# One list of single operations through QKV and W1, tails read by one DMA, and 15 more warm-up transposes

## The chip, the cores and the metric

The kernel runs on one core of one Trainium2 chip. The metric is device time in microseconds (us), the median of several executions. A profiled execution has a span (first to last instruction) and its own time, which is a little longer than the span.

## The reference

S = 2048 tokens, D = 576, F = 4608, all in float32. Two branches read one normalized input and are summed:

```python
xn = _layernorm(x)
return x + _A_ref(xn, A_wqkv, A_wo) + _B_ref(xn, B_w1, B_w2, B_w3, B_w4)
# _A_ref: 32 heads of 18, each token attends to itself and 7 earlier ones, 2 apart
qkv = x @ wqkv                    # 576 -> 1728
o = softmax(q . k * scale) . v    # window of 8, dilation 2
return o @ wo
# _B_ref: spatial shift, then an MLP
h = gelu(layernorm(x) @ w1)       # 576 -> 576, four groups of 144 columns
hs = concat(h[:, g0] shifted +1, g1 shifted -1, g2 shifted +2, g3 shifted -2) @ w2
x1 = x + hs
return x1 + gelu(layernorm(x1) @ w3) @ w4
```

## The kernel before

The stages follow one another on TensorE: QKV, W1 with its GELU, W2, then the MLP (W3 and W4 in turns, with the attention in the background on VectorE), and Wo. A float32 product is made of rounded parts: each operand is split into a high part (ScalarE, a cast) and a remainder (VectorE, a subtraction), and high x high, high x low and low x high are accumulated. D = 576 is four blocks of 128 rows and a tail of 64, or two halves of 288 with tails of 32; the high and low of a tail share one block, so a tail is wanted several times over, at several partitions.

*QKV.* Token tiles 0 to 5 (128 tokens each) go by `unit`, plain products of one tile with 432 columns of `wqkv`: 24 units of 14 matmuls. Each tile is loaded (`x`), its statistics are taken (`st`), it is normalized (`no`, L168), its tails are copied (`ta`, L342), it is turned by TensorE (`tm`, `tt`; L350, L354) and split out of PSUM (`ch`, `cl`, `ct`, `cu`; L553 to L559). The weights come by `load_cg` (`c0.0` to `c3.2`; L304 the halves, L308 the tails), and are split (`wh`, `wl`, `wL`, `wt`, `wu`, `wU`; L323, L326, L524, L528; a capital means GpSimd makes the remainder). Tiles 6 to 15 go in pairs, by 7 products in place of 8 on a 2 x 2 split (`g`, L701); their sums of weight blocks are `sb` (L333), and each pair is turned by VectorE (`zt`), put to memory (`zp`), read back by `get_pair` (`gp`) and split (`sx`, `ph`, `pl`, `pt`, `pu`).

All of this is one string of tokens, `ORDER_Q`. Each token issues the few instructions of one operation, and the loop over it sets each engine's program order. An engine runs its own queue in order, so a token's place matters against the others of its engine. SyncE issues the loads and stores here. Its eight DMA semaphores go round: a DMA waits until the one issued eight before it has landed.

*W1.* After the list stands a loop written by hand: for each of four blocks of 512 tokens, `mix_tile` for each of four column groups (14 matmuls, L785; two GELUs, L790 and L791; the remainder, L792), and `mix_rem`, 9 matmuls for the 64 columns left over (L800), which are copied out (L803), swapped between partitions by eight small DMAs (L805, L806), and placed with their shifts. The normalized blocks lie in memory as `zt`. A ring of two buffers holds them in SBUF; `get_z` loads a block's main rows (L187) and its tail rows (L190), and `split_x` splits it (L218 to L225). Blocks 0 and 1 are loaded from the list. Blocks 2 and 3 are loaded by

```python
            if b + 2 < NB and i == 4:
                get_z(b + 2, ring_block(("z", b + 2)))
```

as the last thing of block b, once its buffer is free. The loop also loads and splits `w2` (L765, L769, L237, L238) and, by `back`, returns five token tiles to SBUF (L656).

*Warm-up.* At the start TensorE turns the identity 24 times (L456), while the first loads are under way.

Of the kernel before, what the change touches and what calls it, by code (L numbers as in the profile page):

```python
# [53 lines left out]
x0 st0 x1 st1 x2 c0.1 st2 no0 ta0 tm0 c0.0 c0.2 x3 c2.0 no1 tm1 no2 c2.1 c2.2 wh0B11.1 wL0B11.1  # L54
wh0B11.0 wl0B11.0 ch0 tt0 ct0 tm2 x4 x5 ch1 st3 u0.0 u1.0 u1.1 cl1 u1.2 zpad cu0 cl0 no3 ta2
wt0B11 wU0B11 ta1a ch2 cl2 tt1 ta3 wh0B12.0 tt2 ct2 ct1 cu1 u0.2 u0.1 u0.3 st4 u0o u0s u1.3 tm3
ch3 cu2 aw3 no4 st5 c1.0 c1.2 c1.1 tt3 ct3 cu3 u2.0 u2.1 x9 tm4 ta4 u1o u1s cl3 wl0B12.0 wt0B12
u2.2 u2.3 u2o ch4 no5 u3.0 u3.1 u2s wh0B12.1 wl0B12.1 x6 u3.2 u3.3 u4.0 u3o u5.0 aw2 tt4 ct4 u3s
u4.1 u4.2 wu0B12 aw1 sb0.0 sb0.1 wh1B11.0 wh1B11.1 tm5 ch5 sc0 u4.3 u4o x7 ta5 wt1B11 u5.1 u5.2 x8
u5.3 u4s u5o u5s sb0.2 wt0T3 sb0.3 st6 no6 u6.0 u6.1 u6.2 u6.3 u6o u6s u7.0 u8.0 u8.1 tt5 u7.1  # L60
u7.2 u7.3 cl4 u8.2 cu4 cl5 u8.3 wh0T3.1 st7 st9 u7o u9.0 st8 wh0T3.0 u9.1 u7s ct5 cu5 u9.2 u9.3
wh0T1.0 u8o u10.0 u9o wl1B11.0 u8s u9s u10.1 u10.2 u10.3 u10o wu0T3 u11.0 u11.1 u11.2 wh0T1.1
u11.3 wl0T3.0 u11o wl1B11.1 u11s u12.0 u12.1 wt0T1 wu1B11 u12.2 u12.3 u12o u13.0 u13.1 u13.2 u10s
no7 wl0T3.1 sc2 wl0T1.1 c3.0 c3.1 wl0T1.0 wu0T1 u14.0 u14.1 u13.3 sc6 u14.2 c3.2 u14.3 u12s early
zg6 zt6 zg7 u13o u15.0 u15.1 u15.2 u15.3 sc8 u13s zt7 zp3.2 wh1B12.0 wh1B12.1 zp3.1 wl1B12.0
wl1B12.1 u14o u16.0 u16.1 u14s wt1B12 zp3.0 zp3.3 sb1.0 wu1B12 sb1.1 sb1.2 sb1.3 u15o u16.2 u15s
wh1T1.0 u17.0 u16.3 u16o wl1T1.0 wh1T3.0 no8 u16s u17.1 u17.2 u18.0 u18.1 u17.3 u17o u18.2 u17s
u18.3 u18o u18s u19.0 u19.1 zg8 zt8 no9 zg9 zt9 u19.2 u19.3 u20.0 u20.1 u20.2 gp3.0 gp3.1 gp3.2
u19o wt1T3 gp3.3 gp3.4 wu1T3 gp3.5 sx3.0 u20.3 u21.0 u21.1 u20o u22.0 wh1T3.1 zp4.0 u21.2 zp4.3
zp4.1 zp4.2 u19s u21.3 pt3A12 pu3A12 u21o ph3A11 pt3A22 pt3A11 sx3.1 sx3.3 ph3S4 pu3A11 pu3A22  # L70
u22.1 u20s u22.2 u22.3 ph3S1 pl3A11 sx3.2 pt3S4 pu3S4 u23.0 u23.1 ph3A22 pl3A22 u23.2 ph3A12 u21s
ph3S3 pl3A12 pl3S4 x10 u23.3 gp4.0 gp4.1 pt3S3 pu3S3 pl3S3 wt1T1 wu1T1 pl3S1 pt3S1 pu3S1 wl1T3.0
wl1T3.1 wh1T1.1 wl1T1.1 st10 x11 st11 no10 gp4.2 gp4.3 gp4.4 u22o u22s gp4.5 sx4.0 u23o u23s mid
g6.1 g6c g7.1 g7c g6.5 g7.5 g6.2 ph4A11 pl4A11 g6o2 g6s2 sx4.2 ph4A12 aw0 g6.6 g6k5 g6k6 g7k5 g7.6
g7k6 g6.7 g6o7 sc10 g6s7 zg10 g6.3 x12 sx4.1 ph4S1 no11 zt10 zg11 g6o3 zt11 zg0 zp5.1 zp5.0 zp5.2
g6.4 g6o4 pt4A11 sc4 g7.7 g6s4 pl4S1 g7o7 zt0 pu4A11 pt4S1 zg1 zt1 pt4A12 pu4A12 sx4.3 g7.3 g7.2
g7o2 g7.4 g7o4 g8.1 g9.1 pu4S1 g8c g8.5 g7o3 g9.5 pt4A22 ph4A22 pu4A22 pt4S3 pl4A22 pl4A12 zg2
zp5.3 zt2 x13 st13 g8.2 st12 sc12 zp0.0 g9c g6s3 g8.6 ph4S3 pl4S3 g8o2 g8k5 g8k6 zp0.1 g7s7 g9k5
g9.6 g9k6 zp0.2 pu4S3 zp0.3 g8s2 no12 no13 g9.3 g9o3 zg12 zt12 zg13 zt13 gp5.0 g8.3 gp5.1 ph5A11
pl5A11 ph5A22 gp5.2 gp5.3 gp5.4 pt5A11 gp5.5 g9.7 pt5A12 g8.7 g9o7 g8o7 g7s4 g7s2 ph5A12 sx5.0 x14  # L80
sx5.1 ph5S1 pu5A12 g9.2 g8.4 x15 g8o4 aw4 g9.4 zp6.1 zg3 pu5A11 g9o2 g9o4 g7s3 pl5A12 zp6.0 g10.1
g11.1 sx5.2 pl5S1 pt5S1 zp6.3 zp6.2 g8s4 g8s7 zt3 zp1.3 g9s7 g8o3 pu5S1 g10c g10.6 st15 g11c g11.6
g8s3 sx5.3 ph5S3 g10.5 st14 sc14 gp6.0 gp6.1 no15 gp6.2 gp6.3 pt5A22 gp6.4 gp6.5 pl5A22 g9s2 no14
# [12 lines left out]
gz1.4 w1l1 g14s4 gz1.5 g15s4 gz1.0 w1h2 gz1.1 gz1.2 gz1.3 g15o3 z0u g15s3 w1h3 w1l3 g14s7 w1l2
# [8 lines left out]
def fused_block(ctx, tc, x, wqkv, wo, w1, w2, w3, w4, out):  # L105
# [75 lines left out]
    def get_z(b, xt, part=None):  # L181
        raw = xt.bitcast(F32)
        for i in range(6):
            if part in (None, i):
                src, c = zt[2 * b + i % 2], slice(256 * (i % 2), 256 * (i % 2) + 256)
                if i > 3:
                    sp.dma_start(raw[:, 5:9, c], src[0:512].rearrange("(k p) c -> p k c", p=128))  # L187
                else:
                    a = 64 * (i // 2)
                    sp.dma_start(raw[a:a + 64, 4, c], src[512:576])  # L190
# [108 lines left out]
    def load_cg(cg, raw, parts=(0, 1, 2)):  # L299
        r = qraw[cg] = raw() if qraw.get(cg) is None else qraw[cg]  # L300
        c = cg * QB
        for k in range(2):
            if k in parts:
                sp.dma_start(r[:, k, 1:3, :], wqkv[HF * k:HF * k + 256, c:c + QB]  # L304
                             .rearrange("(s p) c -> p s c", p=128))
        if 2 in parts:
            for a in range(0, 128, 32):
                sp.dma_start(r[a:a + 32, :, 0, :],  # L308
                             dram_ap(wqkv, 256 * 3 * D + c,
                                     [[3 * D, 32], [HF * 3 * D, 2], [1, QB]]))  # L310
# [62 lines left out]
    def get_pair(p, part):  # L373
        if part < 2:
            k = part
            sp.dma_start(raw_x(p, k)[:, 1:3],
                         dram_ap(zt[p], HF * k * 256, [[256, 128], [128 * 256, 2], [1, 256]]))
        else:
            a = 32 * part - 64
            raw = pair_x(p).bitcast(F32)[:, 0, 512:1024].rearrange("p (k c) -> p k c", k=2)  # L380
            sp.dma_start(raw[a:a + 32],
                         dram_ap(zt[p], 256 * 256, [[256, 32], [HF * 256, 2], [1, 256]]))
# [71 lines left out]
    warm = psa.tile([128, 512], F32, name="p1", tag="a")  # L454
    for i in range(24):
        pe.transpose(warm[:, :128], ident, ident)  # L456
# [38 lines left out]

    for u in range(24):
# [157 lines left out]
    def back():  # L654
        for t in range(5):
            sp.dma_start(Y[:, t, :], ysp[t])  # L656

    for i in range(6):
        add(f"gz0.{i}", lambda i=i: get_z(0, ring_block(("z", 0)), i))
        add(f"gz1.{i}", lambda i=i: get_z(1, ring_block(("z", 1)), i))  # L660

    def split_z(what):
        xt = xring["z", 0]
# [15 lines left out]
    for w in ("t", "u", "h0", "l0", "h1", "l1"):  # L679
        add(f"z0{w}", split_z, w)  # L680
# [59 lines left out]
    for name in ORDER_Q.split():  # L740
        T[name]()
    psq.__exit__(None, None, None)
    open_ab()
    q2p.__exit__(None, None, None)
    qp.__exit__(None, None, None)


    mp = tc.tile_pool(name="mp", bufs=1, reuse_waits="tile")
    mpool = mp.__enter__()
    W2 = mpool.tile([128, 10, D], F32R, name="W2")  # L750
    H = [[mpool.tile([128, S + 4], F32R, name=f"h{p}{g}") for g in range(4)] for p in range(2)]
# [1046 lines left out]
```

## Time and profile before

| | us |
|---|---|
| median of three runs | 1264.47 (1262.1 to 1265.52) |
| profiled execution, its own time | 1261.03 |
| its span | 1259.3 |
| TensorE busy in the span | 1241.0 |
| QKV on TensorE, from the first product matmul | 12.8 to 181.2 |
| W1 | 181.2 to 247.0 |
| W2 and all that follows | 247.0 to the end |
| mean granted TensorE clock | 0.997 |

In a timeline a row is a start, a duration, the engine, the line, the instruction, and in brackets how long the engine stood idle before it and what ended that. SPq is SyncE's queue of DMA issues. Overlapping matmuls are merged, so a group's duration over its count is the step from one to the next. In the table of windows each row is a stretch, its length, and then the busy us and instruction counts of TensorE's matmuls, its weight loads, VectorE, ScalarE and GpSimd, the granted clock, the DMA engines' share and GB/s.

### The profile page before, as it was taken

Reading aid. Unit: us, or ns where it says so; the run is one execution under the profiler, and the core shown is the slowest. Engines: PE = TensorE matmul, PEld = TensorE weight load, DVE = VectorE, ACT = ScalarE, POOL = GpSimd, SP = SyncE. Lnnn points to the kernel's source line nnn. Section 1 sums busy time; section 2 is a strip of 40 time slices with the busy share of each in tenths; the row PEclk is TensorE's granted clock in tenths of the full one; section 3 lists DMA queues with packets and bytes.
Section 4 is the critical chain, followed back from the end, with each engine's and each line's share of the span. In section 5 each row is a group of like instructions: output and inputs, shape, how many; then the busy total and the mean of one; then the engine's idle time right before and its main releaser. Section 6 shows DMA issues by size and latency. Waiting matters only on the chain.

```text
span 1259.3 us, 19957 instructions
## 1 busy us (share of the span) xinstructions
PE 1241.0 (99%) x7346; PEld 1141.6 (91%) x7346; DVE 932.4 (74%) x1182; ACT 759.8 (60%) x1234; POOL 278.7 (22%) x415
## 2 busy tenths in 40 slices
PE   8999999999999999999999999999999999999998
PEld 7999997799898999999899998999989999999898
DVE  6877645678458999997759998989989893554441
ACT  4556565526545545455867777776676776676620
POOL 5503100021222211212223232222122232222200
PEclk8999999999999999999999999999999999999999
DMA  8778993356888986769678898888968769899972
GB/s 221 178 181 200 196 236 111 116 155 177 207 226 183 222 159 145 158 137 246 124 174 188 196 186 210 180 167 212 258 114 186 141 128 199 182 210 232 261 241 78
DMA packets 221130, 230.50 MB, mean 183 GB/s; under 512 B 99544, under 2 KB 158136, under 8 KB 220904
## 3 DMA queue, kind: packets, MB, share of 16 engines
q1 hardware_dynamic: 188280, 162.43, 45.7%
q0 software_dynamic: 32752, 66.80, 32.8%
q8 instruction: 58, 0.95, 0.3%
q14 instruction: 40, 0.33, 0.1%
HBM read 130.76 MB, written 108.82 MB: 190 GB/s over the span
## 4 chain that ended last, share of the span: by engine, by line
PE 65%; DMA 3%; ACT 1%; DVE 1%; issue 1%; SPq 0%; POOL 0%; ACTq 0%; DVEq 0%; POOLq 0%
PE ps L1192 31%; PE cc L1456 19%; PE p L1156 10%; PE ps L252 4%; DMA w3st<-in_B_w_dram 1%; DMA yd<-ev 1%; DMA x1n<-xd 1%; DMA yd<-Y 1%; DVE xt L917 0%; SPq L1492 0%; PE p L1765 0%; DVE Y L1203 0%; ACT Y L1197 0%; ACT Y L1136 0%; DVE w3st L1289 0%
## 5 line engine op out<-in xcount | busy, mean ns | idle before, releaser
L1192 PEld LDWEIGHTS ps<-w,c 128*128 128x128 f32 x3456 | 477.8, 189 | 18.4 <-ACT Y L1197 2.9
L1192 PE MATMUL ps<-w,c 128*128 128x288 f32 x3456 | 487.8, 296 | 3.0 <-ACT Y L1197 1.6
L1198 POOL DMA_DIRECT2D yd<-Y x154 | 138.9, 905 | 369.8 <-ACT Y L1197 315.7
L1147 DVE TENSOR_TENSOR c<-Y,c 128x512 fp32r<-128x512 f32 x144 | 98.9, 687 | 89.2 <-ACT Y L1136 84.4
L1197 ACT COPY Y<-ps 128x576 f32<-128x576 f32 x154 | 97.9, 636 | 74.3 <-PE ps L1192 63.9
L1456 PE MATMUL cc<-xt,w3s 128*128 128x512 f32 (+1 forms) x504 | 127.2, 392 | 0.0
L1456 PEld LDWEIGHTS cc<-xt,w3s 128*128 128x128 f32 (+1 forms) x504 | 92.3, 188 | 17.3
L1200 ACT COPY Y<-ps 128x576 f32<-128x576 f32 x89 | 57.0, 640 | 59.4 <-PE ps L1192 58.0
L1067 DVE TENSOR_TENSOR po<-q,k 128x1152 f32<-128x1152 f32 (+1 forms) x48 | 84.2, 1755 | 0.8
L1070 DVE TENSOR_REDUCE L<-po 128x64 f32<-128x1152 f32 (+1 forms) x48 | 84.0, 1751 | 0.8
L1456 PE MATMUL cc<-x1n,w3a 128*128 128x512 f32 (+1 forms) x336 | 84.6, 392 | 0.0
L1135 ACT ACTIVATE c<-p 128x512 fp32r<-128x512 f32 x48 | 28.7, 598 | 86.3 <-PE p L1156 86.3
L1043 DVE TENSOR_TENSOR po<-v,L 128x1152 f32<-128x1152 f32 x56 | 75.4, 1354 | 0.9
L1466 DVE TENSOR_TENSOR Y<-cc,Y 128x512 f32<-128x512 f32 x49 | 33.7, 688 | 55.4 <-ACT Y L1462 49.7
L434 PE MATMUL p<-wb,xt 128*128 128x432 f32 (+1 forms) x336 | 69.8, 368 | 0.0
L1456 PEld LDWEIGHTS cc<-x1n,w3a 128*128 128x128 f32 (+1 forms) x336 | 60.4, 188 | 10.0
L434 PEld LDWEIGHTS p<-wb,xt 128*128 128x128 f32 (+1 forms) x336 | 64.7, 194 | 2.9
L1047 DVE TENSOR_TENSOR po<-po 128x1152 f32<-128x1152 f32 x49 | 66.4, 1355 | 0.9
L161 POOL TENSOR_TENSOR rs<-rs,mhalf 128x1 f32<-128x1 f32 x32 | 20.2, 632 | 183.8 <-DVE mv L164 106.4
L1173 ACT COPY ps<-Y 128x576 f32<-128x576 f32 x89 | 57.4, 645 | 3.1 <-DVE Y L1203 1.2
L701 PE MATMUL ca<-wb,xt 128*128 128x432 f32 (+1 forms) x280 | 58.4, 359 | 0.0
L701 PEld LDWEIGHTS ca<-wb,xt 128*128 128x128 f32 (+1 forms) x280 | 52.8, 189 | 2.4
(250 smaller groups left out, 2131.0 us busy)
## 6 DMA issues: line engine op xcount, KB each, us to landing
yd<-Y POOLq DMA_DIRECT2D x156, 288.0 KB, 6.2
Y<-in_B_w_dram SPq DMA_DIRECT2D x29, 576.0 KB, 5.7
w3st<-in_B_w_dram SPq DMA_DIRECT2D x56, 256.0 KB, 8.1
qkvd<-stg SPq DMA_DIRECT2D x44, 216.0 KB, 4.0
yd<-ev POOLq DMA_DIRECT2D x26, 288.0 KB, 6.8
w3st<-in_B_w_dram SPq DMA_DIRECT2D x92, 64.0 KB, 7.6
xd<-big SPq DMA_DIRECT2D x16, 320.0 KB, 6.9
Y<-in_A_x_dram SPq DMA_DIRECT2D x16, 288.0 KB, 4.9
```

Source lines behind the costliest of these rows:

```text
L434: pe.matmul(ps[:, :QB], xo[:n, o + k, a, :], W[:n, w + k, v, :], start=i == 0, stop=i == len(PLAIN) - 1)
L701: pe.matmul(ps, form(g // 2, x, n, a), W[:n, OP[w], v, :], start=start and i == 0, stop=stop and i == len(HALVES) - 1, skip_group_check=True)
L1043: dve.tensor_tensor(dst, vv, Lf[:, :, w:w + 1].to_broadcast([128, TPP * GH, HD]), op=ALU.mult)
L1047: dve.tensor_tensor(o, o, dst, op=ALU.add)
L1067: dve.tensor_tensor(dst, qf[:, None, :].to_broadcast([128, n, TPP * GC]), win, op=ALU.mult)
L1070: dve.tensor_reduce(Lw[:, w:w + n, :], dst.rearrange("p w (x d) -> p w x d", d=HD), axis=AX.X, op=ALU.add)
L1147: dve.tensor_tensor(h[:, 1, :], g, h[:, 0, :].bitcast(F32), op=ALU.subtract)
L1156: pe.matmul(ps, W3[f][:, w, :], x1n[b][:, a, :], start=n == 0, stop=n == len(PAIRS) - 1)
L1192: pe.matmul(ps[:, k, :HF], h[:, col], w[:, p, k * HF:(k + 1) * HF], start=n == 0 and not seed, stop=n == len(seq) - 1, skip_group_check=True)
L1197: act.copy(e.rearrange("p (h c) -> p h c", h=2), ps[:, :, :HF])
L1198: pool.dma_start(yd[t], e, accum_op=ALU.add)
L1456: pe.matmul(ps, WX[w][:k, v, SLOT[w], :], area[sb][xk][:k, a, :], start=onto is None and i == 0, stop=last and i == len(HALVES) - 1, skip_ ...
```

## The change

Three things are done.

1. *One list.* W1's loop is taken apart into single operations with tokens (`m` a product in two parts, `mh`, `mg`, `ml` its two GELUs and remainder, `r`, `ro`, `rs`, `rg`, `rp` the left-over columns, `gz` and `z` a block's load and split, `vr`, `vh`, `vl` the split of `w2`, `bk` a returned tile, `hz` the zeroed margins), and the whole string through QKV and W1 has a new order. The token `seam` closes QKV's buffers and opens W1's. A product takes those row blocks of x first that the first half of the split gives, and the GELU's float32 copy `g32` has two buffers where it had one.
2. *Tails.* A tail that is wanted several times over is read by one DMA a block, with a stride of 0 for the repeats, in place of two or four DMAs: two for four in `load_cg` and `get_pair`, two for four in `get_z`, one for two for `w1`, four for eight for `w2`.
3. *Warm-up.* Tokens `pw0` to `pw4` in the list add three transposes of the identity each. The tile that they write moves to the pool of the turned tiles.

The diff; of the string only a row before and a few after stand here, and of W1's operations those that the words above don't tell:

```diff
 ORDER_Q = """
-x0 st0 x1 st1 x2 c0.1 st2 no0 ta0 tm0 c0.0 c0.2 x3 c2.0 no1 tm1 no2 c2.1 c2.2 wh0B11.1 wL0B11.1
...
+x0 pw0 st0 x1 st1 no0 ta0 tm0 x2 st2 c0.0 c0.1 pw1 pw2 x3 c0.2 pw3 ch0 tt0 c2.0 c2.1 c2.2 wh0B11.0
...
-    def get_z(b, xt, part=None):
+    def get_z(b, xt, part):
         raw = xt.bitcast(F32)
-        for i in range(6):
-            if part in (None, i):
-                src, c = zt[2 * b + i % 2], slice(256 * (i % 2), 256 * (i % 2) + 256)
-                if i > 3:
-                    sp.dma_start(raw[:, 5:9, c], src[0:512].rearrange("(k p) c -> p k c", p=128))
-                else:
-                    a = 64 * (i // 2)
-                    sp.dma_start(raw[a:a + 64, 4, c], src[512:576])
+        src, c = zt[2 * b + part % 2], slice(256 * (part % 2), 256 * (part % 2) + 256)
+        if part < 2:
+            sp.dma_start(raw[:, 5:9, c], src[0:512].rearrange("(k p) c -> p k c", p=128))
+        else:
+            sp.dma_start(raw[:, 4, c], dram_ap(src, 512 * 256, [[0, 2], [256, 64], [1, 256]]))
...
         if 2 in parts:
-            for a in range(0, 128, 32):
-                sp.dma_start(r[a:a + 32, :, 0, :],
-                             dram_ap(wqkv, 256 * 3 * D + c,
-                                     [[3 * D, 32], [HF * 3 * D, 2], [1, QB]]))
+            for k in range(2):
+                sp.dma_start(r[:, k, 0, :], dram_ap(wqkv, (256 + HF * k) * 3 * D + c,
+                                                    [[0, 4], [3 * D, 32], [1, QB]]))
...
-    warm = psa.tile([128, 512], F32, name="p1", tag="a")
-    for i in range(24):
-        pe.transpose(warm[:, :128], ident, ident)
+    warm = psb.tile([128, 2, 512], F32, name="ps", tag="b")
+
+    def warm_up(n):
+        for _ in range(n):
+            pe.transpose(warm[:, 0, :128], ident, ident)
+
+    warm_up(24)
...
-    for name in ORDER_Q.split():
-        T[name]()
...
+    def margin(i):
+        t = H[i % 2][i // 2] if i < 8 else T4
+        for c in ((0, 2), (S + 2, S + 4)) if i < 8 else ((0, 4), (S, S + 4)):
+            pool.memset(t[:, c[0]:c[1]].bitcast(F32), 0.0)
...
-        for i, (a, w) in enumerate(PAIRS):
+    def mix(b, m, n0, n1):
+        if n0 == 0:
+            mps[b, m] = psb.tile([128, 2, 512], F32, name="ps", tag="b")[:, 0, :]
+        xt, ps = xring["z", b], mps[b, m]
+        for i, (a, w) in list(enumerate(sorted(PAIRS, key=lambda s: s[0] % 5 in (2, 3))))[n0:n1]:
             pe.matmul(ps, W1[:, w, m * 128:(m + 1) * 128], xt[:, a, :],
                       start=i == 0, stop=i == len(PAIRS) - 1)
...
     for b in range(NB):
-        for i, m in enumerate((0, 1, 2, 4, 3) if b < 3 else (4, 0, 1, 2, 3)):
...
+        for m in range(4):
+            add(f"m{b}{m}.0", mix, b, m, 0, 8)
+            add(f"m{b}{m}.1", mix, b, m, 8, 14)
+            for w in "hgl":
+                add(f"m{w}{b}{m}", mix_leave, b, m, w)
+        add(f"r{b}", rem, b)
...
+    for name in ORDER_Q.split():
+        T[name]()
```

How the change moves instructions, at the three places that the prediction speaks of. (L numbers of before and of the changed kernel differ: L456, L350, L354, L434 are L464, L357, L361, L440 there.)

TensorE at the start: warm-up transposes of `ident`, turns of `Y`, and the first units. Before:

```order
L456 MATMUL p_154<-ident 128x128 x24
L350 MATMUL ps<-ident,Y 128x128 x8
L354 MATMUL ps<-ident,Y 128x128 x2
L350 MATMUL ps<-ident,Y 128x128 x4
L434 MATMUL p_253<-wb_125,xt 128x432 x6
L434 MATMUL p_260<-wb_125,xt 128x432 x12
L354 MATMUL ps<-ident,Y 128x128 x4
L434 MATMUL p_253<-wb_125,xt 128x432 x8
```

Now:

```order
L464 MATMUL ps<-ident 128x128 x27
L357 MATMUL ps<-ident,Y 128x128 x4
L464 MATMUL ps<-ident 128x128 x9
L361 MATMUL ps<-ident,Y 128x128 x2
L357 MATMUL ps<-ident,Y 128x128 x4
L464 MATMUL ps<-ident 128x128 x3
L357 MATMUL ps<-ident,Y 128x128 x4
L440 MATMUL p_271<-wb_125,xt 128x432 x6
L440 MATMUL p_279<-wb_125,xt 128x432 x12
```

Fifteen transposes stand among the first turns, and unit 1 still follows unit 0's first six matmuls.

SyncE at the start: token tiles (`Y`), weight halves (128x2x432) and weight tails. Before:

```order
L278 DMA Y<-in_A_x_dram 128x576 x3
L304 DMA rawa<-in_A_wqkv_dram 128x2x432 x2
L308 DMA rawa<-in_A_wqkv_dram 32x2x432 x4
L278 DMA Y<-in_A_x_dram 128x576
L304 DMA rawb<-in_A_wqkv_dram 128x2x432 x2
L308 DMA rawb<-in_A_wqkv_dram 32x2x432 x4
```

Now:

```order
L286 DMA Y<-in_A_x_dram 128x576 x3
L312 DMA rawa<-in_A_wqkv_dram 128x2x432 x2
L286 DMA Y<-in_A_x_dram 128x576
L316 DMA rawa<-in_A_wqkv_dram 128x1x432 x2
L312 DMA rawb<-in_A_wqkv_dram 128x2x432 x2
L316 DMA rawb<-in_A_wqkv_dram 128x1x432 x2
```

Tile 3 goes ahead of the first tails, and each block's tails are two DMAs.

SyncE in W1, from the swaps of block 0's left-over columns (`v<-u`) to the loads of block 2 (`zt_115`, `zt_116`: its two halves). Before:

```order
L805 DMA v<-u 16x512
L806 DMA v<-u 16x512
L805 DMA v<-u 16x512
L806 DMA v<-u 16x512
L805 DMA v<-u 16x512
L806 DMA v<-u 16x512
L190 DMA xt<-zt_115 64x256
L190 DMA xt<-zt_116 64x256
L190 DMA xt<-zt_115 64x256
L190 DMA xt<-zt_116 64x256
L187 DMA xt<-zt_115 128x4x256
```

Now:

```order
L840 DMA v<-u 16x512 x2
L797 DMA Y<-ysp_182 128x576
L840 DMA v<-u 16x512
L781 DMA w2r<-in_B_w_dram 128x576
L842 DMA v<-u 16x512
L196 DMA xt<-zt_115 128x4x256
L196 DMA xt<-zt_116 128x4x256
L198 DMA xt<-zt_115 128x1x256
L198 DMA xt<-zt_116 128x1x256
```

Four of the eight swaps, one returned tile and one load of `w2` stand ahead of block 2's loads, whose large parts come first; the other four swaps follow later.

More of the change, by code (lines that the diff above doesn't have):

```diff
@@ L72 @@
[L72 to L83, printed above, removed]
@@ L494, in unit_spill @@
         spill(ust[u], t, cg * QB, QB)
+    for i in range(16):
+        add(f"pw{i}", warm_up, 3)
     for u in range(24):
@@ L652, in fused_block, with split_z @@
         add(f"w1l{m}", split_w1, m, 1)
[L654 to L663, printed above, removed]
+    for b in range(NB):
+        for i in range(4):
+            add(f"gz{b}.{i}", lambda b=b, i=i: get_z(b, ring_block(("z", b)), i))
+    def split_z(b, what):
+        xt = xring["z", b]
         raw = xt.bitcast(F32)
@@ new lines, in rem, with rem_out, rem_swap @@
+    def rem(b):
+        ps = mps[b] = psb.tile([128, 2, 512], F32, name="ps", tag="b")[:, 0, :]
+        for a in range(9):
+            pe.matmul(ps, W1R[:, a if a < 5 else a - 5, :], xring["z", b][:, a, :],
+                      start=a == 0, stop=a == 8)
+    def rem_out(b):
+        uv[b] = [mupool.tile([128, 512], F32, name=n, bufs=2) for n in "uv"]
+        act.copy(tokens(uv[b][0]), turned_order(mps[b]))
+    def rem_swap(b, i):
+        u, v = uv[b]
+        q = 32 * (i // 2)
+        if i % 2 == 0:
```

230 lines of the change are left out of this document (123 added, 107 removed).

## The prediction

> **What bounds the kernel now.** I read the page's busy shares first, then the table of windows, then the list of what TensorE waited for, and last the timeline of two places.
>
> ```profile
> PE 1241.0 (99%) x7346; PEld 1141.6 (91%) x7346; DVE 932.4 (74%) x1182; ACT 759.8 (60%) x1234; POOL 278.7 (22%) x415
> ```
>
> ```profile
> 20.00:40.00 20.00, 19.23 (x105) 18.10 (x104) 17.08 (x28) 11.40 (x19) 7.01 (x12) 1.00 0.95 246
> 40.00:60.00 20.00, 20.00 (x104) 19.10 (x104) 15.65 (x26) 9.39 (x15) 15.46 (x24) 1.00 0.50 124
> 60.00:80.00 20.00, 20.00 (x104) 19.16 (x103) 14.48 (x15) 10.33 (x17) 0.30 (x1) 1.00 0.78 171
> 80.00:100.00 20.00, 20.00 (x103) 19.15 (x102) 17.68 (x37) 13.01 (x29) 6.91 (x16) 1.00 0.75 183
> ```
>
> TensorE is busy for 1241.0 of 1259.3 us, and the change removes no matmul. So nothing can come but from the 18.3 us in which it stood idle, and from matmuls that ran slowly. The windows (TensorE, weight loads, VectorE, ScalarE, GpSimd, clock, DMA) show the first stage dense from 40 us on, and VectorE behind it at 72 to 88 per cent. Idle time sits at the two ends of what the new list covers: the first 24 us, and the W1 stage at 181 to 247 us.
>
> The start, TensorE alone (timeline; start, duration):
>
> ```profile
> 1.38 5.38 PE L456 MATMUL p<-ident 128*128 128x128 f32 x24 [1.38 <-POOL ident masks.py:199]
> 8.64 1.15 PE L350 MATMUL ps<-ident,Y 128*128 128x128 f32 x8 [1.89 <-DVE Y L168]
> 11.67 0.66 PE L354 MATMUL ps<-ident,Y 128*128 128x128 f32 x2 [1.88 <-POOL wb L326]
> 12.12 1.06 PE L350 MATMUL ps<-ident,Y 128*128 128x128 f32 x4
> 12.84 5.91 PE L434 MATMUL p<-wb,xt 128*128 128x432 f32 x18
> 22.34 0.41 PE L354 MATMUL ps<-ident,Y 128*128 128x128 f32 x2 [0.77 <-POOL rs L161]
> 22.51 1.81 PE L434 MATMUL p<-wb,xt 128*128 128x432 f32 x8
> 24.52 6.53 PE L434 MATMUL p<-wb,xt 128*128 128x432 f32 x32
> ```
>
> and its granted clock (sixth figure after the stretch's length):
>
> ```profile
> 3.90:7.30 3.40, 2.86 (x14) 2.45 (x12) 2.72 (x10) 0.00 (x0) 1.12 (x2) 1.00 0.88 262
> 7.30:10.70 3.40, 1.15 (x8) 0.85 (x8) 2.29 (x7) 1.49 (x2) 2.52 (x3) 1.00 1.07 276
> 10.70:14.10 3.40, 2.43 (x10) 2.37 (x11) 2.64 (x6) 2.56 (x6) 0.89 (x1) 0.50 1.06 333
> 14.10:17.50 3.40, 3.40 (x11) 3.13 (x10) 3.36 (x5) 1.53 (x3) 2.95 (x3) 0.50 1.02 243
> 17.50:21.00 3.50, 3.50 (x22) 3.29 (x21) 1.68 (x5) 0.85 (x3) 0.40 (x1) 0.99 0.07 27
> ```
>
> The first matmul of the product waits until 12.84, and 18 of them take 5.91 us, 328 ns each, where later 32 take 6.53 us, 204 ns each. In the stretch with 1.15 us of work in 3.4 the clock was lost: 0.50 for the next 6.8 us, and back only after a full stretch. That cost 18 x 124 ns = 2.2 us beside the 1.9 + 1.9 + 0.8 us of waits.
>
> In the W1 stage, what TensorE waited for between 180 and 262 us (total, times, longest):
>
> ```profile
> PE ps L800 <- ACT g L791: 1.8, 1, 1.8
> PE ps L785 <- DVE xt L225: 1.2, 1, 1.2
> PE ps L785 <- ACT g L791: 1.1, 1, 1.1
> PE ps L800 <- DVE xt L225: 0.9, 1, 0.9
> PE ps L800 <- ACT xt L224: 0.2, 1, 0.2
> ```
>
> Sum 5.2 us. All five are one thing, twice: the block after next arrives late.
>
> ```profile
> 192.93 3.33 PE L785 MATMUL ps<-xt,W 128*128 128x512 f32 x14
> 201.00 2.44 SPq L190 DMA_DIRECT2D xt<-zt  x4
> 203.48 1.19 SPq L187 DMA_DIRECT2D xt<-zt  x2
> 209.48 1.05 ACT L224 CAST xt<-xt 128x1024 fp32r<-128x1024 f32 x1 [2.20 <-DMA xt<-zt]
> ```
>
> The 14 matmuls of the first row are block 0's last; they end at 196.3. But SyncE issues block 2's tails at 201.0, behind eight swaps of 16 rows, and its two large loads at 203.5. They land for ScalarE's cast at 209.48, which stands in ScalarE's queue ahead of the GELUs that free the accumulators.
>
> **The start, step by step.** What decides there, on the other engines:
>
> ```profile
> 3.12 2.40 SPq L308 DMA_DIRECT2D rawa<-in_A_wqkv_dram  x4
> 6.85 0.82 DVE L158 BATCH_NORM_STATS2 bn<-Y 128x6 f32<-128x288 f32 x2 [0.41 <-DMA Y<-in_A_x_dram]
> 8.01 1.71 DVE L168 TENSOR_SCALAR Y<-Y,mv,rs 128x576 f32<-128x576 f32 x3
> 8.04 0.91 ACT L323 CAST wb<-rawa 128x864 fp32r<-128x864 f32 x1 [6.01 <-DMA rawa<-in_A_wqkv_dram]
> 9.31 2.28 POOL L326 TENSOR_TENSOR wb<-rawa,wb 128x864 fp32r<-128x864 f32 x1
> 10.13 0.91 ACT L323 CAST wb<-rawa 128x864 fp32r<-128x864 f32 x1 [1.18 <-DMA rawa<-in_A_wqkv_dram]
> 11.07 1.43 DVE L326 TENSOR_TENSOR wb<-rawa,wb 128x864 fp32r<-128x864 f32 x1 [1.35 <-ACT wb L323]
> 13.11 0.92 ACT L524 CAST wb<-rawa 96x864 fp32r<-96x864 f32 x1
> 15.14 2.05 POOL L528 TENSOR_TENSOR wb<-rawa,wb 32x864 fp32r<-32x864 f32 x1
> 30.00 1.59 DVE L333 TENSOR_TENSOR rawa<-rawb,rawa 128x1296 f32<-128x1296 f32 x1
> ```
>
> VectorE's norm of token tile 0 moves ahead of tile 2's statistics, which waited until 6.85 for their data. So the first turn comes at about 7.0 instead of 8.64, right behind the 27 warm-up transposes. The nine after it last 9 x 144 ns (the row at 8.64) to 9 x 224 ns (the first row), 1.3 to 2.0 us. They lie in a wait that is still there, since the second half of the first weight block lands at about 10.1 as before. If that cover were gone, they would cost that much. The last three cost at most 0.7 us ahead of the same wait. The 1.15 us of work in the third clock stretch become almost 3.4, and I take the clock to stay at 1.00.
>
> At 10.1 ScalarE casts the second weight half, to 11.04. The other half, landed at 8.0, has its remainder made by VectorE before that (it ran at 11.07), so the products start at 11.1 instead of 12.84. GpSimd's remainder (2.28) then ends at 13.35, and its tail remainder (2.05), with one small operation between, at about 16.0. VectorE's turned tails follow, and I get the first two units and four turned tiles done at 17.75. Before, that point is 22.51, where the third unit starts. TensorE's own work fits: 28 matmuls at 204 ns are 5.7 us of the 6.65 between; at 328 ns they would be 9.2. The lead is 4.8 us.
>
> VectorE then takes 0.4 of it. Its first sum of weight blocks (1.59) now stands ahead of tile 2's casts, where it stood at 30.00, and my walk along its queue has unit 3 wait until 23.8 for the tail of its tile. Unit 3 ends at 24.3 so, against 28.7 before (22.51, 28 matmuls at the 192 ns of the dense windows, 20.00 over 104, and six transposes at 144 ns). **Start: 4.4 us.** Bounds: 1.2 (only the clock held to 14.1, ten matmuls) and 6.8 (2.2 plus all three waits). I take the walk, as each step of it has a row.
>
> The tail loads: two issues for four of 2.40 us, 1.2 us less on SyncE a block. Nothing waited for SyncE here but later loads, so 0 is counted.
>
> **QKV's middle.** Every operation has the same shape and all move. TensorE was fully busy, so the gain is 0. A loss is possible where VectorE has too little left: it is free for 4.35 + 5.52 us of 40 to 80, and 4.4 us less time leaves 5.5. I count 0, and keep up to 2 for the range.
>
> **The W1 stage.** After block 0 there are now six issues ahead of block 2's loads, four of them swaps, all issued while TensorE is still at block 0, and the large loads go first. So they go out 0 and 0.6 us after block 0 instead of 7.2 and 7.8, and with the same 6 us to land they are there some 7 us before block 2's first matmul, which follows block 0 by 65 matmuls, 14.3 us at about 0.22. ScalarE's first cast now stands behind block 1's third GELU, which ends some 9.9 us after block 0; cast (1.05) and remainder (about 1.2) are done at 12.2, 2 us ahead of need. The products also take the first half block first. **Gain 5.2 us, all the waits**; bounds 0 and 5.2. The margins' small memsets (GpSimd, almost idle here), the weight splits and the reload of five tiles (SyncE, behind block 2's loads but for one) move within those engines' spare time. The order of the stages behind is unchanged, so they only start earlier.
>
> **Sum:** 4.4 + 5.2 = 9.6 us. From the profiled execution (span 1259.3, its own time 1261.03) that gives 1251.4; from the median of the three runs, 1264.47, it gives 1254.9. I take 1253.5, because one low run is weak evidence for the level, and a lost clock may be part of why the others are longer.
>
> **The rivals.**
>
> *The clock is not held.* Then 10.7 to 17.5 stays at 0.50 and the 28 matmuls need their 328 ns; two units end at about 20.3, and a start gain of 2 is left: 7.2 in all, 1256. Against it stands the row at 8.64: eight turns in 1.15 us after 24 transposes alone, against 224 ns each before, so transposes did raise the clock. The Trainium skill, "TensorE: Matmul & The Clock Gate", Part 4, says that the full clock does not engage for transposes, as they do not count as busy; by that rule this rival is the result, and the trace does not bear it out.
>
> *The lead at the start is eaten*, VectorE being at 85 per cent of 20 to 40 us and 88 of 80 to 100: only W1's 5.2 remain, 1258.
>
> *W1 still waits*, its loads or ScalarE's order being late in another place: 4.4 remain, 1259.
>
> *Nothing net*: what the two ends give is lost in QKV's middle, or the list does not do what it says: 1263.
>
> *Slower: the pair loads.* Each pair of token tiles in QKV goes to memory and back:
>
> ```profile
> zt<-zst SPq DMA_DIRECT2D x24, 144.0 KB, 3.6
> xt<-zt SPq DMA_DIRECT2D x10, 256.0 KB, 4.1
> ```
>
> SyncE runs in order, and the new list puts these issues elsewhere. If at each of the five pairs TensorE waited for one load, 5 x 4.1 = 20.5 would be lost, and 1274 results; from 1.9 us a pair on the change is slower. Before, none of them showed in the dense windows, and the list still issues pair 4's loads before the last products of the pair ahead of it.
>
> **How the numbers follow.** Forecast 0.58 (1250.5 to 1256), clock not held 0.12, lead eaten 0.10, W1 still waits 0.08, nothing net 0.07, pair loads 0.05. The range 1249.5 to 1259.5 holds the first four but for their edges and leaves out the last two. 0.3 per cent, 3.8 us, is about what a measurement of this kernel can tell from no change (its three runs spread by 3.4 us); so below 1260.7 counts as faster: 0.58 + 0.12 + 0.10 + 0.06 = 0.86. Same 0.10, slower 0.04.
>
> **What would show it.** The first pair products of QKV stand here before:
>
> ```profile
> 84.46 2.94 PE L701 MATMUL ca<-wb,xt 128*128 128x432 f32 x14
> ```
>
> In the profile after: clock 1.00 from 7.3 us on; the first product matmul at 11 us, the third unit at 17.8, the fifth at 24.2; the pair products, in the row above at 84.46, at 80; under 0.5 us of waits of TensorE in the W1 stage; the stages behind unchanged in length. It is wrong if TensorE waits again between 25 and 175 us, or if a clock of 0.50 stands behind 10 us.

## The result, and the profile after

| | before | changed |
|---|---|---|
| median, us | 1263.28 (4 runs, 1261.86 to 1265.52) | 1276.03 (4 runs, 1273.39 to 1277.46) |
| ratio | | 1.0097, 95% interval 1.0072 to 1.0121 |
| profiled execution: own time, span | 1261.03, 1259.3 | 1276.6, 1274.8 |

The changed kernel is 12.75 us slower. The page's line of busy times, of the changed kernel:

```profile
PE 1249.9 (98%) x7361; PEld 1147.1 (90%) x7361; DVE 930.7 (73%) x1182; ACT 760.3 (60%) x1234; POOL 284.0 (22%) x415
```

TensorE is busy 8.9 us longer with the same products and 15 more transposes, and it stands idle 24.9 us in place of 18.3. Most of the first is the clock: by the trace's clock records behind the first 8 us and up to the last matmul it was 0.50 for 20.5 us, before for 6.8; 13.7 us more at half speed cost up to 6.8 us (an estimate). The second are waits. What TensorE waited for, in the whole run (total, times, longest):

```profile
PE ps L1223 <- ACT Y L1228: 4.8, 4, 3.4
PE p L440 <- DVE xt L567: 3.4, 1, 3.4
PE ps L829 <- ACT g L822: 2.6, 1, 2.6
PE ps L812 <- ACT stg L728: 2.5, 1, 2.5
PE ca L710 <- DVE xt L422: 2.1, 1, 2.1
PE p L1187 <- ACT Y L1167: 1.8, 1, 1.8
```

Before, no wait was longer than 1.9 us. The table of windows of the changed kernel shows the start, and two stretches further on:

```profile
7.30:10.70 3.40, 3.27 (x27) 2.99 (x26) 2.92 (x7) 2.99 (x5) 1.94 (x3) 1.00 1.05 299
10.70:14.10 3.40, 3.11 (x17) 2.56 (x15) 1.17 (x4) 0.00 (x0) 1.90 (x2) 1.00 0.37 112
14.10:17.50 3.40, 0.27 (x1) 0.27 (x2) 1.02 (x2) 2.71 (x5) 1.67 (x1) 0.80 0.67 229
17.50:21.00 3.50, 3.50 (x12) 3.07 (x13) 2.92 (x4) 0.62 (x2) 1.19 (x3) 0.50 0.44 164
190.00:194.00 4.00, 4.00 (x12) 3.11 (x12) 3.94 (x7) 2.55 (x3) 0.00 (x0) 0.57 0.72 214
241.40:244.80 3.40, 3.40 (x10) 2.62 (x9) 2.71 (x5) 1.15 (x2) 0.00 (x0) 0.50 0.00 0
```

The clock now holds to 16.1 us, as forecast. But from 10.7 to 14.1 the sixteen DMA engines are busy for 37 per cent, where they were at 106 before (the row at 10.70 in the prediction), with loads outstanding all the while. ScalarE does nothing there (0.00). Then TensorE does almost nothing (0.27 of 3.40 us), and the clock is 0.50 from 16.1 to 22.9 us. Behind the later long waits it is 0.50 for 3.4 us each, from 166.3, 190.2, 241.4 and 1193.7. The same place in the timeline:

```profile
3.64 1.33 SPq L316 DMA_DIRECT2D rawa<-in_A_wqkv_dram  x2
6.53 4.47 SPq L316 DMA_DIRECT2D rawb<-in_A_wqkv_dram  x2
14.79 0.91 ACT L536 CAST wb<-rawa 96x864 fp32r<-96x864 f32 x1 [4.49 <-DMA rawa<-in_A_wqkv_dram]
17.23 1.81 PE L440 MATMUL p<-wb,xt 128*128 128x432 f32 x4 [3.42 <-DVE xt L567]
```

The cast of the first block's tail starts at 14.79, 1.7 us later than before (13.11), though its two DMAs were issued at 3.64. ScalarE stands for 4.5 us in front of it. And SyncE needs 4.47 us to issue the two tails of the next block.

The beginning of W1, of the changed kernel:

```profile
171.15 2.53 SPq L198 DMA_DIRECT2D xt<-zt  x1
174.01 2.53 SPq L428 DMA_DIRECT2D qkvd<-stg  x1
176.64 0.96 SPq L255 DMA_DIRECT2D Y<-in_B_w_dram  x1
185.82 1.98 ACT L658 CAST W<-Y 128x640 fp32r<-128x640 f32 x3 [3.22 <-DMA Y<-in_B_w_dram]
189.76 2.57 PE L812 MATMUL ps<-xt,W 128*128 128x512 f32 x6 [2.50 <-ACT stg L728]
```

A tail of block 0, issued at 171.15, holds SyncE for 2.53 us, and so does the spill behind it. So the load of `w1` goes out at 176.64; ScalarE waits for it until 185.82; the copies behind its casts, which free TensorE's accumulators, are late, and so is W1.

The other two waits of TensorE between 25 and 250 us, and what ScalarE stood for ahead of the first:

```profile
156.08 0.62 ACT L728 ACTIVATE stg<-cb,mv 128x432 f32<-128x432 f32 x1 [5.32 <-DMA qkvd<-stg]
165.24 0.47 PE L710 MATMUL ca<-wb,xt 96*128 96x432 f32 x1 [2.11 <-DVE xt L422]
239.94 1.39 PE L829 MATMUL ps<-xt,W1R 128*128 128x512 f32 x5 [2.62 <-ACT g L822]
```

At 156.08 ScalarE had waited 5.32 us for an ordinary store of `stg`. It went out at 145.69, right behind `w1`'s tail, and landed 10.3 us later; pair 7's casts stand behind such copies in ScalarE's queue. At 241 it is block 3's second tail, issued at 225.64 and landed at 235.33. ScalarE waits 1.96 us for it, and the GELUs that free the accumulators come behind its cast.

When each DMA landed is worked out from the trace: its issue, and the rises of its semaphore up to the last. "Rises" is how many there were for one DMA.

```
                                before                  changed
c0's tails, issued 3.1 to 4.9   16 rises, last 12.29    5 rises, 12.69 and 14.71
c2's tails                      16 rises, last 18.00    5 rises, 19.23 and 21.59
block 0's tails, us to land     16 rises, 5.8 to 7.9    3 rises, 7.8 and 10.1
block 1's tails, us to land     16 rises, 3.0 to 5.8    3 rises, 7.7 and 10.5
w2's tails (4 now)                                      3 rises, 4.5 to 6.8
```

Only the DMAs that read with a stride of 0 have 5 or 3 rises. The first of them mostly comes 1 us after the issue, while an ordinary load's first comes 2 to 6 us after. So I take one rise to be none of data, and 4 or 2 to be data's. The tails with 4 repeats have 4, those with 2 repeats have 2.

The packets in the traces say the same. From 12.3 to 14.2 us, with both c2 tails and one or two of c0's outstanding, 4 packets are in flight for four fifths of the time and never more than 6, nearly all of 1728 bytes (a row of 432 numbers). So these tails share the same four engines. In the run with sixteen repeats (the last one below) 16 or more packets are in flight from 10.7 to 14.1. From 175.0 to 175.6, with block 0's two tails outstanding, 2 packets of 1024 bytes are in flight for most of the time. That is the theory to test: **the tail runs on as many DMA engines as it has repeats, and holds up what stands behind it there.**

The Trainium skill says it in "DMA: Bandwidth & Descriptors", "Why a DMA increments its semaphore by 16 and not by 1": a DMA issued as here runs on the largest number of engines, up to 16, that divides the slowest dimension of both sides, each engine raises the semaphore once, and the sequencer writes the rest at once. Its "Rules for kernel authors" name a leading stride of 0 with c copies as a case that keeps the DMA to at most c engines. The 5 and 3 rises agree.

### The profile page after: what moved, and what is told of

Same layout as the page of the kernel before. It is cut to its first block, busy times and chain, and to the rows that moved or that the text cites. A ratio compares the mean times of both kernels' runs of the same rounds, so it can differ in the third digit from the quotient of the medians.

```text
span 1274.8 us, 19925 instructions
## 1 busy us (share of the span) xinstructions
PE 1249.9 (98%) x7361; PEld 1147.1 (90%) x7361; DVE 930.7 (73%) x1182; ACT 760.3 (60%) x1234; POOL 284.0 (22%) x415
## 5 line engine op out<-in xcount | busy, mean ns | idle before, releaser
L1223 PEld LDWEIGHTS ps<-w,c 128*128 128x128 f32 x3456 | 479.3, 189 | 22.5 <-ACT Y L1228 6.3
L1223 PE MATMUL ps<-w,c 128*128 128x288 f32 x3456 | 489.8, 296 | 6.5 <-ACT Y L1228 4.8
L1178 DVE TENSOR_TENSOR c<-Y,c 128x512 fp32r<-128x512 f32 x144 | 98.7, 687 | 81.1 <-ACT Y L1167 75.9
L440 PE MATMUL p<-wb,xt 128*128 128x432 f32 (+1 forms) x336 | 70.3, 368 | 3.4 <-DVE xt L567 3.4
L440 PEld LDWEIGHTS p<-wb,xt 128*128 128x128 f32 (+1 forms) x336 | 64.1, 193 | 6.6 <-DVE xt L567 3.7
L710 PE MATMUL ca<-wb,xt 128*128 128x432 f32 (+1 forms) x280 | 61.2, 366 | 2.5 <-DVE xt L422 2.1
```

The lines of the kernel that those rows point to most:

```text
L440: pe.matmul(ps[:, :QB], xo[:n, o + k, a, :], W[:n, w + k, v, :], start=i == 0, stop=i == len(PLAIN) - 1)
L710: pe.matmul(ps, form(g // 2, x, n, a), W[:n, OP[w], v, :], start=start and i == 0, stop=stop and i == len(HALVES) - 1, skip_group_check=True)
L1178: dve.tensor_tensor(h[:, 1, :], g, h[:, 0, :].bitcast(F32), op=ALU.subtract)
L1223: pe.matmul(ps[:, k, :HF], h[:, col], w[:, p, k * HF:(k + 1) * HF], start=n == 0 and not seed, stop=n == len(seq) - 1, skip_group_check=True)
```

## The experiments

Where TensorE was, in us of each profile (start of the matmul; worked out from the traces). Single profiles of one kernel differ by some 2 us at the start already, since the loads there land differently. The profiled execution took 1277.1 us with QKV's weight tails old and 1260.83 with only them new, 4.7 and 3.7 above the medians.

```
                          third  first  pairs   W1      W1      last    median
                          unit   pair   end     start   end     matmul  (ratio to before)
before                    22.5   84.5   181.0   181.2   246.8   1255.1  1262.4 to 1264.5
changed                   22.6   84.8   186.9   189.8   255.3   1270.8  1276.03 (1.0097)
all tails old             20.4   84.9   184.4   184.6   243.3   1251.5  1256.13 (0.9941)
old list, tails new       26.7   91.0   190.5   198.7   275.7   1283.0  1291.88 (1.0228)
QKV's weight tails old    18.8   82.5   186.2   188.2   254.5   1271.2  1272.41 (1.0079)
all old, no transposes    17.6   81.1   180.5   180.7   239.5   1248.5  1255.67 (0.9934)
only QKV's weights new    22.8   85.0   184.9   185.1   243.8   1255.0  1257.16 (0.9940)
old list in QKV           22.0   83.9   180.5   181.1   240.8   1249.0  1255.95 (0.9938)
only z, w1, w2 new        18.4   82.0   183.6   187.4   252.9   1262.9  1269.67 (1.0053)
only pairs new            18.2   81.6   180.2   180.3   239.1   1248.0  1256.17 (0.9940)
old tails, together       19.1   82.7   179.8   180.0   238.8   1249.7  1255.05 (0.9935)
16 repeats, all           17.6   79.8   176.8   177.0   235.8   1246.5  1251.95 (0.9914)
```

**All tails old, the rest of the change kept.** The edit, and its like for the pairs, W1's blocks, `w1` and `w2`:

```diff
-            for k in range(2):
-                sp.dma_start(r[:, k, 0, :], dram_ap(wqkv, (256 + HF * k) * 3 * D + c,
-                                                    [[0, 4], [3 * D, 32], [1, QB]]))
+            for a in range(0, 128, 32):
+                sp.dma_start(r[a:a + 32, :, 0, :], dram_ap(wqkv, 256 * 3 * D + c,
+                                                           [[3 * D, 32], [HF * 3 * D, 2], [1, QB]]))
```

> The changed kernel with all five kinds of tail loads in their old form (two or four DMAs for each part, 32 or 64 rows each, no stride of 0); the new list and the 15 transposes stay. Theory A, the tails: all that was lost comes from the repeated reads, which land late (c0's two at 12.7 and 14.7 us, block 0's at 196 and 200). Then c0's tails land by about 12.8, the third unit starts at 18 to 20 instead of 22.56, W1 begins before 179 instead of 189.76, and the time is 1250 to 1258. Theory B, the list: the new order itself starves TensorE around 166, 190 and 241 us, and the late tails only add to it. Then the waits at pair 7 and at the start of W1 stay, W1 begins after 184, and the time is 1265 to 1273. The late stalls at 321 and 1189 us are in neither theory's sum; they go if they come from what ran before, and stay if they were there by chance of timing (up to 5 us more).

1256.13 us, ratio 0.9941 (0.9926 to 0.9955): theory A. No wait of TensorE is left in W1, which takes 58.8 us in place of 65.6, and all clocks are 1.00. c0's tails landed at 13.0 to 15.1 in this profile, the third unit came at 20.42, and W1 began at 184.57, later than theory A said. Most of that is this execution's start: its first pair came at 84.9, where the other kernels with old weight tails and the new start have 81.1 to 82.7. Beside it, two waits at 93 and 101 us stood in the way:

```profile
PE cc L713 <- ACT keep L720: 1.0, 1, 1.0
PE ca L713 <- DVE keep L734: 0.7, 1, 0.7
```

**The old list with only the tails new.** The same edit the other way round, in the kernel before.

> The kernel before with its own order and warm-up, and only the repeated tail reads of the change (QKV's weight blocks, the pairs, blocks 0 to 3 of W1, w1 and w2). Theory A, the tails: the start loses 2 to 4 us, and what needs a tail soon (a pair's sums, W1's first block) waits; 1267 to 1280. Theory B, the list: with the old order nothing waits long for a tail, and the time is that of before, 1261 to 1266.

1291.88 us, ratio 1.0228 (1.0213 to 1.0242): theory A, and more than its 1280. The tails do harm without the new list, and more than with it: the old list has `w1`'s tail right behind two of block 0's, and with 2 repeats each they stand on the same engines: rows of `w1`'s (2304 bytes) go at two at a time once block 0's (1024 bytes) have ended at 189.0, and `w1`'s lands 15.8 us after its issue. What it held up, between 155 and 205 us:

```profile
ACT W L643 <- DMA Y<-in_B_w_dram: 10.7, 1, 10.7
PE ps L781 <- ACT stg L716: 7.8, 1, 7.8
```

**Is it the count or the stride of 0?** Two kernels change one number each in `load_cg`:

```diff
-  (256 + HF * k) * 3 * D + c, [[0, 4], [3 * D, 32], [1, QB]]
+  (208 + HF * k) * 3 * D + c, [[16 * 3 * D, 4], [3 * D, 32], [1, QB]]     # four runs
+  (256 + HF * k) * 3 * D + c, [[0, 16], [3 * D, 8], [1, QB]]              # sixteen repeats
```

> The changed kernel, with QKV's weight tails read as four overlapping runs of 32 rows, 16 rows apart, in place of four times the same rows: the same shape, an outermost count of 4, but no stride of 0. It leaves out the right rows: three quarters of each tail hold other rows of the weights, so the product is not the reference's. Theory A1, an outermost count of 4 keeps a DMA on few engines: each tail finishes with 5 updates and c0's tails land at about 12.7 and 14.7 us as in the changed kernel; third unit at 22.5, time 1274 to 1278. Theory A2, it is the repeated reading of the same addresses: 16 updates or not, the tails land by 12.8 and the time is 1270 to 1274.

> The changed kernel with QKV's weight tails read as 16 repeats of 8 rows in place of 4 repeats of 32: a stride of 0, but an outermost count of 16. It leaves out the right rows: each tail holds the first 8 of its 32 rows sixteen times, so the product is not the reference's. If the outermost count decides: 16 updates for each tail, c0's tails landed by 13.6 us, and a start as with the old weight tails (third unit at 18 to 20.5; 1270 to 1274). If the stride of 0 is slow by itself: the tails land at 12.7 and 14.7 or later, third unit at 22.5, 1274 to 1278.

Four runs without a stride of 0: 5 rises, landed at 12.26 and 14.38, third unit at 21.7, 1272.42 us in one run. Rises, landings and (to 0.8 us) the start are as the first theory has them. The time lies in the second theory's range, 1 us below the lowest of the changed kernel's four, and one run does not decide it. Sixteen repeats with a stride of 0: 16 rises, 11.66 and 12.59, third unit at 18.7, 1271.74, also one run. The windows of the four runs and then of the sixteen repeats, at the place where the changed kernel had a DMA share of 0.37:

```profile
10.70:14.10 3.40, 3.12 (x17) 2.57 (x15) 1.18 (x4) 0.00 (x0) 1.91 (x2) 1.00 0.34 123
```

```profile
10.70:14.10 3.40, 3.40 (x18) 2.83 (x16) 1.69 (x5) 1.86 (x5) 2.67 (x3) 1.00 1.07 277
```

The outermost count decides how the tails land, the stride of 0 does not matter there.

**QKV's weight tails alone old, and alone new.**

> The changed kernel with only the tails of QKV's weight blocks in their old form; the pairs, the blocks of W1, w1 and w2 keep the repeated reads. Theory A, the tails: the start is as with all tails old (third unit at 18 to 20), the lead of 3 to 5 us lasts to 140, and the waits at 165 and 190 us remain, so 1270 to 1274. Theory B, the list: little moves, 1274 to 1277.

> The changed kernel with the old tails for the pairs, the blocks of W1, w1 and w2; only QKV's weight tails are read with repeats. The other way round (only those old) gave 1272.4, 3.6 us less than all new; all old gave 1256.1. If the losses add up: 1256.1 + 3.6 = 1259.7 (1258 to 1262), with the wait of about 3 us and the clock of 0.50 behind 16 us at the start, and no wait over 1.5 us between 150 and 250 us. If a late start is what makes the later loads late: waits again near 165 and 190 us, and 1264 to 1272.

1272.41 and 1257.16. Taking these tails away from the changed kernel lowers the median by 3.6 us (ratio 1.0060 to 1.0098, against 1.0072 to 1.0121), and putting them alone into the kernel with old tails raises it by 1.0. The intervals tell neither from nothing. With them old, the third unit comes at 18.8, and the waits at W1's start remain. The start with them alone shows the same hole as the changed kernel (the row at 14.10, where TensorE works 0.04 us), but no wait of TensorE stands between 150 and 250 us:

```profile
10.70:14.10 3.40, 3.40 (x19) 2.87 (x17) 1.50 (x5) 0.00 (x0) 2.23 (x2) 1.00 0.54 129
14.10:17.50 3.40, 0.04 (x1) 0.00 (x0) 0.18 (x1) 1.87 (x4) 0.83 (x1) 1.00 0.66 231
```

So a late start does not make the later loads late. 1257.16 is less than the 1258 to 1262 of losses that add up, but with 3.6 as unsure as it is, that is not shown.

**Only the blocks of W1, `w1` and `w2` new; only the pairs new.**

> The changed kernel with the old tails for QKV's weights and for the pairs; the blocks of W1, w1 and w2 keep the repeated reads (outermost count 2). All old gave 1256.1, all new 1276.0, only QKV's weights new 1257.2. If the count of 2 is the costly kind: W1 starts 3 to 6 us later than with all old (184.57), W1 takes 64 to 66 us in place of 58.8, and the time is 1265 to 1274. If the pairs' tails (count 4) were what cost: no wait in W1 and 1256 to 1260.

> The changed kernel with the old tails for QKV's weights, the blocks of W1, w1 and w2; only the pairs keep the repeated reads (outermost count 4). If the waits at 165 us come from pair 7's tails: the pair products again lose 3 to 5 us between matmuls 294 and 490, W1 itself takes 59 us, and the time is 1257 to 1261. If the pairs' tails are harmless and it is the late z tails that hold them up: no loss there, and 1253 to 1256, since the two waits at 93 and 101 us seen with the old pair tails go.

1269.67 and 1256.17. The tails with two repeats are the costly kind: 13.5 of the 19.9 us between all old and all new. Their waits, the first at W1's start, the second behind block 3's tails:

```profile
PE ps L814 <- ACT stg L730: 3.5, 1, 3.5
PE ps L831 <- ACT g L824: 3.2, 1, 3.2
```

The pairs' tails alone cost nothing that these runs can tell, and the waits at 93 and 101 us are gone with them. The three parts alone make 13.5, 1.0 and 0.0, or 14.6 of the 19.9; whether the rest comes of their meeting or of noise is not shown.

**Those two waits.** In the old form each DMA holds 32 partitions of both halves, so that the first cast of pair 4 needs both parts, and the new list puts the second far behind the first. The edit moves the second up:

```diff
-... gp4.2 wl1T3.0 wt1T1 wu1T1 x11 ph3S4 ... x10 u22s wh1T1.1 wl1T1.1 pt3S3 gp4.3 ...
+... gp4.2 gp4.3 wl1T3.0 wt1T1 wu1T1 x11 ph3S4 ... x10 u22s wh1T1.1 wl1T1.1 pt3S3 ...
```

> The changed kernel with all tails in their old form, and in the list the second pair of a pair's tail DMAs moved up to stand right behind the first (16, 27 and 22 places for pairs 4, 6 and 7). With the old form each DMA holds 32 partitions of both halves, so pair 4's first cast needs both parts, where with the repeated form it needed only one. If that is the cause of the waits at 93 and 101 us (1.0 and 0.7 us, and 2.2 us in all between pair products 0 and 98): they go, and the time is 1253 to 1254.5. If VectorE or ScalarE is late there for another reason: 1255.5 to 1257.

The waits went, and from the first pair to the last QKV takes 97.1 us in place of 99.5. The median is 1255.05, ratio 0.9935 (0.9914 to 0.9956): lower than 1256.13, but the intervals overlap, and it lies between the two ranges expected. It has the lowest median of the kernels that leave nothing out.

**The transposes, and the two halves of the list**, both with old tails:

> The changed kernel with all tails in their old form, as in the run with all old tails (1256.1 us, clock 1.00 throughout, third unit at 20.42), and without the 15 transposes of the list. If the transposes hold the clock and this counts: a clock of 0.50 for 6.8 us somewhere between 10 and 25 us, and 1258 to 1260. If the clock is lost but the start waits for data in any case: the 0.50 shows, and the time stays within 1 us of 1256. If the clock is held without them: neither.

> All tails old; the list is that of before as far as the end of QKV (so without the 15 transposes), and that of the changed kernel through W1. With all tails old, the new QKV list reached W1 3.4 us later than before in one profile, and its W1 then won 6.8. If the QKV half of the list really loses 3.4 us and the W1 half wins 6.8: W1 starts at 181 to 182, and the time is 1262.6 - 6.8 - 1 to 1262.6 - 6.8 + 1, so 1255 to 1257, below or at the run with the whole new list. If that 3.4 us is only what one execution differs from another and the new QKV list wins at the start: 1258 to 1262, since W1's gain is then smaller than it looked.

Without the 15 transposes 1255.67, and the clock held:

```profile
7.30:10.70 3.40, 2.30 (x15) 2.03 (x16) 2.92 (x7) 2.92 (x5) 2.01 (x2) 1.00 1.07 256
10.70:14.10 3.40, 3.19 (x17) 2.65 (x17) 2.07 (x6) 2.60 (x5) 3.32 (x3) 1.00 1.08 288
```

TensorE works 2.30 us of the stretch in which it worked 1.15 before, because the norm of tile 0 comes sooner (its turns start at 6.52, before at 8.64). The transposes add nothing to the time that the intervals can tell. With the old list in QKV 1255.95: W1's part of the list gives the gain, W1 taking 59.7 us in place of 65.6, and QKV's part gives nothing that these runs can tell (1256.13 and 1255.05 with it).

**The changed kernel with one number changed in each tail read.** The same list, the same issues and bytes:

```diff
-[[0, 4], [3 * D, 32], [1, QB]]   [[0, 4], [256, 32], [1, 256]]   [[0, 2], [256, 64], [1, 256]]
+[[0, 16], [3 * D, 8], [1, QB]]   [[0, 16], [256, 8], [1, 256]]   [[0, 16], [256, 8], [1, 256]]
-[[0, 2], [D, 64], [1, D]]        [[0, 2], [D, 16], [1, D]]
+[[0, 16], [D, 8], [1, D]]        [[0, 16], [D, 2], [1, D]]
```

> The changed kernel to the letter of its list and its number of DMAs, with one number changed in each of the five tail reads: 16 repeats where there were 4 or 2 (of 8 rows, 2 for w2), so the same bytes, a stride of 0 and one issue a block, but an outermost count of 16. It leaves out the right rows: the tails hold the first 8 (or 2) rows again and again, so the result is not the reference's. If the count alone made the loss: the wait at W1's start and the clock of 0.50 behind it go, W1 takes 59 us, and the time is 1252 to 1257, as with the old tails. If fewer, larger issues, or reading the same rows again and again, also cost: 1262 or more. If fewer issues are worth something by themselves: below the 1255.0 of the old tails put together, 1250 to 1253.

1251.95 us, ratio 0.9914 (0.9889 to 0.9938): 24 us below the changed kernel. The same places as above, in this run's timeline:

```profile
10.80 0.92 ACT L536 CAST wb<-rawa 96x864 fp32r<-96x864 f32 x1 [0.51 <-DMA rawa<-in_A_wqkv_dram]
161.26 0.66 SPq L198 DMA_DIRECT2D xt<-zt  x1
164.37 1.08 SPq L255 DMA_DIRECT2D Y<-in_B_w_dram  x1
177.00 3.38 PE L812 MATMUL ps<-xt,W 128*128 128x512 f32 x14
```

The tail's cast runs at 10.80 in place of 14.79, SyncE's issue takes 0.66 us in place of 2.53, and W1 starts without a wait. In the 4 us from 190 on there are 19 matmuls at full clock, where the changed kernel had 12. All its tails have 16 rises. Whether fewer issues are worth the 3 us between this and the old tails put together is not settled: the intervals overlap, and this kernel reads 8 rows (2 for `w2`) again and again where the right tails read 32, 64 or 16, which was not tried apart.

## Why the prediction was wrong

**The step that failed** is "The tail loads: two issues for four of 2.40 us, 1.2 us less on SyncE a block. Nothing waited for SyncE here but later loads, so 0 is counted." It counted issues, and took the landing as it was; the W1 step said so too ("the same 6 us to land"). Both were wrong. The tails of QKV's weights and of W1's blocks landed 6.5 to 13.4 us after their issue, each on 4 or 2 engines, and SyncE's share rose: of its issues in the first 255 us, 20 took more than 1.5 us, against 4 before and 2 with sixteen repeats. What waited was not only later loads: ScalarE stood for the tails, and for what came behind them on SyncE, ahead of the copies that TensorE needs. The step had no upper bound from any row, and the range none for it.

**The other steps** are seen in the run with sixteen repeats, which is the change without its fault, though with wrong rows in the tails.

- *Start, 4.4 us.* There 4.7 at the first pair, with the third unit at 17.6 (forecast 17.75) and the fifth at 23.9 (24.2). That is in part luck: the first product came at 9.7, not 11.1, as the two weight halves landed at 6.7 and 7.9 in that execution (8.0 and 10.1 before), and the first two units then took 7.9 us in place of 6.65. The six profiles with old weight tails and the new start give 3.4 (without the transposes), 2.8, 2.4, 1.9, 1.8 and -0.5, 2.0 in the mean, all against one profile of before. So the size is what the best execution gives, and about twice the mean. With old tails the medians do not show it: 1255.95 with the old list in QKV, 1256.13 and 1255.05 with the new.
- *The clock.* With sixteen repeats it was 1.00 throughout, so the rival failed; but the reason given, the transposes, was not the cause, as the run without them shows. The third stretch did fill up, by products and turns that came sooner.
- *QKV's middle, 0.* From the first pair to the last 97.0 us, against 96.5 before. Right.
- *W1, 5.2 us.* 58.8 us against 65.6: 6.8. The mechanism was right, no wait is left; the gain is 1.6 us more than the list of waits held and than the upper bound of 5.2, and where these come from is not shown.
- *The sum, 9.6.* 11.0 at W1's end, and the median 10.5 below its comparison, without the tails' fault. With it, the 9.6 turned into a loss of 12.75.

**The rivals.** "Slower: the pair loads" gave 1274, near the time measured, but it is not what happened: with only the pairs' tails new nothing is lost. A wait at pair 7 did come where it looked for them, but it takes more than the pairs' tails: `w1`'s tail, with 2 repeats, is issued among pair 7's at 145.04 and landed 9.9 us later, and the store behind it is what ScalarE stood for. TensorE's wait there is 2.1 us with all tails new, 1.0 with only the blocks', `w1`'s and `w2`'s, and none with only the pairs'. The two signs that the prediction named for being wrong both came: a wait of 2.1 us at 165, and a clock of 0.50 from 16.1 to 22.9.

**Open.** Of the 15.7 us by which the changed kernel's profile is behind at the last matmul, 8.5 are there at W1's end; 2.4 came at 321 us (the wait for L1167 in the list above) and 5.6 behind 1185 (L1223), in stages that the change doesn't touch. The second loss shows in other kernels too, by 0 to 3.6 us, with old tails as well (3.6 with only QKV's weights new, 2.6 with sixteen repeats). No run isolates it. Nor was it tried why SyncE's issue grows longer when the engines in question are loaded, only that it does.

## What to carry to other kernels

Before merging DMAs, look at the outermost count of the merged access: here 4 or 2 repeats in front made a 128-partition transfer run on 4 or 2 of 16 engines, and 12.75 us were lost where the same list with several DMAs a tail won 6.5 (1256.13 against 1262.59). Several DMAs of 32 or 64 rows each were better than one. One DMA with an outermost count of 16 ran on all 16 here, but no kernel of this case has that with the right rows. In a trace such a DMA is known by few rises of its semaphore, by a low DMA share while loads are outstanding, and by issues of SyncE that take microseconds.

## What the runs showed of the hardware that was not expected

- A DMA confined to few engines also slows those that use all: the two large loads between c0's tails and c2's landed 10.8 and 11.4 us after their issue, against 6.7 and 7.7 with the same list and sixteen repeats. And it holds up the queue that issues: 4.47 us for two.
- In the changed kernel each of the five waits of TensorE of 2.1 to 3.4 us went with a clock of 0.50, for 6.8 us at the first and 3.4 us at the others; behind the wait of 1.8 us at 321 it stayed at 1.00. In the row at 190 this costs 7 matmuls, 1.5 us, on top of the wait. At the start, working 2.30 of 3.4 us kept the clock and working 1.15 lost it.
